# The first batch of an FFT mixing kernel: all filter pieces on one DMA queue in order of use, own tiles for split evacuations, fill work on TensorE

## The chip, the cores and the metric

The kernel runs on one core of one Trainium2 chip. The metric is the device time of one launch in microseconds (us); lower is better.

The engines go by short names. In this kernel TensorE (PE in the profiles) does the matmuls, ACT and DVE (ScalarE and VectorE) do element-wise work, GpSimd (POOL) does side work, and SP only issues transfers (DMA). The matmuls write their results to tiles in PSUM, a memory whose parts are called banks; an **evacuation** is the copy of such a tile out of PSUM by ACT or DVE. The **granted clock** (PEclk) is the share of its full clock that TensorE was given.

## The reference

```python
# x: 8 x 3008 x 256; 24064 tokens in all
X = np.fft.rfft(x, axis=1)
Y = X * (filt_r + 1j * filt_i)[None, :, :]
y = np.fft.irfft(Y, n=3008, axis=1)
# feed-forward over all tokens, d_ff = 2048
h = y.reshape(24064, 256) @ w_in
g = h * (1.0 / (1.0 + np.exp(-beta * h)))
out = g @ w_out
```

## The kernel before

The kernel does the FFT as matmuls over 3008 = 47 x 64. A batch goes through stage 1 (`s1`), a turn by transposes (`a0_turn`), stage 2 (`s2`), the product with the filters, stage 3 (`s3`), a second turn (`z_turn`) and stage 4 (`s4`; in pieces of four columns `f_0`). Batches 1 to 7 go through in small pieces while TensorE works on the feed-forward matmuls of the batch before. Batch 0 has nothing to hide behind. Its stages, and the tables that they need, make up the **opening**, which ends when the first feed-forward matmul, `hps`, starts. The change touches only the opening.

In the opening, six units of eight frequency rows by 128 channels pass through these functions. Most of these are a group of matmuls on TensorE and an evacuation of the PSUM tile by ACT or DVE (in `s2_0` the products on DVE take the evacuation's place). In the traces (Code shortened, cuts marked with dots.)

```python
spsum = pool("spsum", bufs=3, PSUM)     # tiles of two banks
tpsum = pool("tpsum", bufs=2, PSUM)     # tiles of one bank
def bank2(shape, dt=F32): return spsum.tile(shape, dt, ...)
def turn8(): return tpsum.tile([P, KH, P], BF16, ...)

def evac(dst, src, on_act, scale=None):   # ACT if on_act, else DVE
    ...

def z_turn(e, hh, on_act):                # a0_turn is built alike
    tp = turn8()
    for i in range(KH):
        nc.tensor.transpose(tp[:, i, :], zT[e][:, j0 : j0 + P], ident[:])
    evac(zz0[:, hh * KH : (hh + 1) * KH, e * P : (e + 1) * P], tp[:KP], on_act)

def s2_0(n):                              # ... 8 matmuls into ps = bank2(...)
    for c, filt in enumerate((fr_sb, fi_sb)):
        nc.vector.tensor_tensor(r_t[:], ps[:], filt[:, ks, ds], ALU.mult)
        pq[n, c] = r_t                    # the "filter products"

def s3_0(n, split=False):
    ps = bank2([P, KH, P])
    ...                                   # 8 matmuls with t3, 8 with t3s
    if split:
        for h in range(2):                # two engines, ONE tile
            evac(dst[:, js], src[:, js], h == 1)
    else:
        evac(dst, src, True)

def f_0(e, u, on_act):                    # 4 matmuls into a tpsum tile, then evac to y
    ...
def spread(n):                            # GpSimd copies a filter piece to the other half
    nc.gpsimd.tensor_copy(fr_sb[M:, ks, ds], fr_sb[:M, ks, ds])
    nc.gpsimd.tensor_copy(fi_sb[:M, ks, ds], fi_sb[M:, ks, ds])
```

The end of the opening, in program order:

```python
s2_0(4)
a0_turn(2, 1, True)
z_turn(0, 0, True); z_turn(0, 1, True)
s3_0(3); s2_0(5)
f_0(0, 0, True); f_0(0, 1, True)
z_turn(0, 2, True); z_turn(0, 3, True)
f_0(0, 2, True); f_0(0, 3, True)
s3_0(4)
f_0(0, 4, True); f_0(0, 5, True)
s3_0(5, True)                              # split
f_0(0, 6, False); f_0(0, 7, True)
z_turn(1, 0, False); z_turn(1, 1, True)
z_pair(1, 2, (False, True))
s4_0(1, 0, False); s4_0(1, 1, True); s4_0(1, 2, False); s4_0(1, 3, True)
# then the steady state: hps, gT, acc, and the plan of the later batches, e.g.
for g in range(4):
    at(o + 14 + 3 * g, load_x, 2, g)       # x of batch 2, by steps of hps
```

## Time and profile before

| | |
|---|---|
| median of 3 runs | 788.2 us (787.86 to 788.35) |
| span of the profiled run | 786.9 us |
| first filter product starts | 18.75 us |
| last filter product ends | 35.32 us |
| first `hps` starts (end of the opening) | 44.52 us |
| last group on TensorE starts | 780.99 us |

The page of the kernel before: the span, the busy time of each engine, and the chain of work that ended last by engine.

```profile
span 786.9 us, 15233 instructions
...
PE 771.1 (98%) x6063; PEld 547.6 (70%) x6063; DVE 438.1 (56%) x686; ACT 562.3 (71%) x827; POOL 155.6 (20%) x162
...
PE 95%; ACT 2%; DVE 1%; DMA 1%; issue 0%; ACTq 0%
```

TensorE (PE) is the limit over the span, and between 100 and 700 us it is busy for 599.8 of 600 us. A change of the opening therefore pays only by an earlier first `hps`, and it pays in full as long as nothing later waits.

The windows of the kernel before, three stretches of the opening. After the stretch come its length, the busy time of each engine with its instructions, the mean granted TensorE clock (PEclk, 1.00 is full), the share of DMA and the rate.

```profile
core 0: us, PE busy (x) PEld busy (x) DVE busy (x) ACT busy (x) POOL busy (x), PEclk, DMA share, GB/s
17.00:19.00 2.00, 1.85 (x19) 1.69 (x18) 2.00 (x3) 1.72 (x3) 1.94 (x3) 0.50 1.26 255
34.00:36.00 2.00, 1.91 (x20) 1.91 (x20) 1.33 (x2) 0.90 (x3) 1.94 (x4) 0.50 1.10 223
36.00:38.00 2.00, 2.00 (x29) 2.00 (x27) 0.00 (x0) 1.69 (x3) 2.00 (x2) 0.66 1.02 205
```

In all three TensorE looks busy, but at half clock or, in the third, two thirds.

The timeline of the kernel before. The columns are start and busy time in us, engine, line, operation, output and inputs, and how many instructions; in brackets the idle time just before and what ended it.

```profile
start us, us, engine line op out<-in xcount [idle before <-releaser]
...
16.53 2.29 DVE L292 TENSOR_SCALAR t3s<-t,rot 128x512 bf16<-128x512 bf16 x2
18.75 1.21 DVE L434 TENSOR_TENSOR pq_t<-sps,fr_sb 128x1024 bf16<-128x1024 f32 x1
...
28.19 1.93 ACT L113 ACTIVATE zz<-tps 96x1024 bf16<-96x1024 bf16 x2
28.36 0.61 PE L397 MATMUL tps<-ident,zT 128*128 128x128 bf16 x8 [0.29 <-ACT a L113]
...
34.11 1.21 DVE L434 TENSOR_TENSOR pq_t<-sps,fi_sb 128x1024 bf16<-128x1024 f32 x1
34.36 1.06 PE L443 MATMUL sps<-t,pq_t 128*128 128x128 bf16 x8
...
37.47 0.61 PE L443 MATMUL sps<-t3s,pq_t 128*128 128x128 bf16 x8
38.12 0.69 DVE L115 CAST zT<-sps 128x512 bf16<-128x512 f32 x1 [2.79 <-PE sps L443]
38.84 0.60 ACT L113 ACTIVATE zT<-sps 128x512 bf16<-128x512 f32 x1 [0.76 <-DVE zT L115]
...
44.52 0.59 PE L732 MATMUL hps<-y,win_sb 128*128 128x512 bf16 x2 [0.70 <-DVE y L117]
...
65.65 0.38 PE L594 MATMUL ps<-a,t 128*128 128x256 bf16 x2 [1.22 <-DMA a<-d]
```

DVE spends 2.29 us on two table rotations just before the first product. The group of eight matmuls at 34.36 us takes 1.06 us at a granted clock of 0.50; the one at 37.47 us, where the clock is back (1.00 from 37.5 us on), takes 0.61. The two halves of the last split evacuation run one after the other although they are on two engines: ACT waits 0.76 us for DVE. The last group of stage 3 (37.47 us, inputs `t3s,pq_t`) starts 2.15 us after the last product has ended, and from there it takes 7.05 us to `hps`. And in the steady state there is a wait of 1.22 us for a load.

The chain of work that ended last, three of its pieces, from the kernel before (start and length in us, what):

```profile
26.37 1.03 ACT zT L113
...
27.45 0.64 PE tps L397 x8
...
28.19 1.93 ACT zz L113 x2
```

From 17.53 to 44.52 us this chain passes through ACT's evacuations and the TensorE groups between them, and near the end through evacuations on DVE.

### The profile page before, as it was taken

How to read it: one execution, taken by the hardware profiler on the slowest of the kernel's cores; microseconds unless marked ns; L12 is line 12 of the kernel's file. 1: busy time of each engine (PE TensorE's matmuls, PEld its weight loads, DVE VectorE, ACT ScalarE, POOL GpSimd, SP SyncE). 2: the span in 40 equal slices, each digit the busy share in tenths (PEclk: the TensorE clock that was granted, in tenths of full speed). 3: DMA queues.
4: the chain of work that ended last, by engine and by line, in shares of the span. 5: the costliest groups of instructions: out<-in, count | busy, mean ns of one | idle time of the engine just before them, and what ended most of it. 6: DMA issues, size and time to landing. Idle time of an engine off the chain costs nothing.

```text
span 786.9 us, 15233 instructions
## 1 busy us (share of the span) xinstructions
PE 771.1 (98%) x6063; PEld 547.6 (70%) x6063; DVE 438.1 (56%) x686; ACT 562.3 (71%) x827; POOL 155.6 (20%) x162
## 2 busy tenths in 40 slices
PE   7799999999999999999999999999999999999997
PEld 5766767766677666876678666786667766776665
DVE  8746844776556665566655676466655566320101
ACT  6887867667666766767667776677766777777776
POOL 7823400232002220121201222012200222000000
PEclk9899999999999999999999999999999999999999
DMA  9959286233931348223480326713164211500101
GB/s 187 226 152 206 69 234 154 76 95 79 243 109 48 87 128 224 77 70 105 111 253 28 99 84 143 211 41 101 49 187 108 75 47 48 155 28 27 55 27 54
DMA packets 87066, 88.50 MB, mean 112 GB/s; under 512 B 5628, under 2 KB 77820, under 8 KB 86996
## 3 DMA queue, kind: packets, MB, share of 16 engines
q1 hardware_dynamic: 82420, 72.37, 31.1%
q0 software_dynamic: 4576, 15.17, 11.2%
q8 instruction: 47, 0.77, 0.4%
q14 instruction: 23, 0.19, 0.1%
HBM read 54.47 MB, written 46.66 MB: 129 GB/s over the span
## 4 chain that ended last, share of the span: by engine, by line
PE 95%; ACT 2%; DVE 1%; DMA 1%; issue 0%; ACTq 0%
PE acc L752 42%; PE hps L732 41%; PE ps L578 3%; PE ps L645 2%; PE ps L594 2%; PE ps L623 2%; DMA a<-d 1%; PE tps L268 1%; PE sps L443 1%; ACT zT L113 0%; ACT zz L113 0%; DVE aT L115 0%; PE tps L397 0%; DVE y L117 0%; PE tps L274 0%
## 5 line engine op out<-in xcount | busy, mean ns | idle before, releaser
L741 ACT ACTIVATE gT<-hps,beta_sb 128x512 bf16<-128x512 f32 x752 | 517.0, 687 | 208.7 <-PE hps L732 206.1
L752 PE MATMUL acc<-wout_sb,gT 128*128 128x256 bf16 x3008 | 453.4, 272 | 0.0
L732 PE MATMUL hps<-y,win_sb 128*128 128x512 bf16 (+7 forms) x1728 | 448.0, 351 | 0.9 <-DVE y L117 0.7
L752 PEld LDWEIGHTS <-gT 128*128 128x128 bf16 x3008 | 287.6, 98 | 126.1 <-issue 1.2
L613 POOL TENSOR_TENSOR yh<-a_t,b_t 128x512 bf16<-128x512 f32 x84 | 106.4, 1266 | 421.9 <-DVE b_t L612 421.0
L732 PEld LDWEIGHTS <-win_sb 128*128 128x128 bf16 x1728 | 164.9, 98 | 25.0 <-issue 1.0
L115 DVE COPY ost<-acc 128x512 f32<-128x512 f32 x93 | 59.9, 685 | 146.9 <-PE acc L752 146.9
L115 DVE CAST a<-ps 96x512 bf16<-96x512 f32 x104 | 70.8, 685 | 51.9 <-PE ps L578 47.9
L608 DVE TENSOR_TENSOR a_t<-ps,fr_sb 128x512 f32<-128x512 f32 x84 | 58.1, 692 | 72.4 <-PE ps L594 71.4
L117 DVE TENSOR_SCALAR y<-ps 128x376 bf16<-128x376 f32 x104 | 56.0, 548 | 59.3 <-PE ps L645 59.1
L609 DVE SCALAR_TENSOR_TENSOR b_t<-ps,fi_sb 64x512 f32<-64x512 f32 x84 | 58.2, 692 | 1.1
L612 DVE TENSOR_TENSOR b_t<-ps,fi_sb 64x512 f32<-64x512 f32 x84 | 57.4, 683 | 1.1
L115 DVE CAST z<-ps 128x512 bf16<-128x512 f32 x72 | 49.3, 684 | 1.7 <-PE ps L623 0.8
L645 PEld LDWEIGHTS <-zz 96*128 96x128 bf16 x448 | 29.8, 98 | 22.9
L578 PE MATMUL ps<-xg,t 94*96 94x512 bf16 x112 | 41.5, 381 | 0.0
L645 PE MATMUL ps<-t,zz 96*128 96x94 bf16 x448 | 34.7, 205 | 0.0
L594 PE MATMUL ps<-a,t 128*128 128x256 bf16 x168 | 32.1, 273 | 1.2 <-DMA a<-d 1.2
L623 PE MATMUL ps<-yh,t 128*128 128x256 bf16 x168 | 32.1, 273 | 0.0
L623 PEld LDWEIGHTS <-t 128*128 128x128 bf16 x168 | 16.3, 98 | 17.7
L594 PEld LDWEIGHTS <-t 128*128 128x128 bf16 x168 | 16.1, 98 | 16.6 <-issue 1.5
L173 POOL DMA_DIRECT2D xg<-in_x_dram x24 | 12.4, 519 | 56.5 <-PE ps L578 56.5
L578 PEld LDWEIGHTS <-t 94*96 94x96 bf16 x112 | 13.8, 123 | 10.5
(104 smaller groups left out, 194.8 us busy)
## 6 DMA issues: line engine op xcount, KB each, us to landing
out_dram<-ost SPq DMA_DIRECT2D x46, 512.0 KB, 3.0
d<-a SPq DMA_DIRECT2D x28, 384.0 KB, 4.5
a<-d SPq DMA_DIRECT2D x28, 384.0 KB, 5.5
d<-z SPq DMA_DIRECT2D x28, 384.0 KB, 3.7
zz<-d SPq DMA_DIRECT2D x28, 384.0 KB, 6.5
xg<-in_x_dram POOLq DMA_DIRECT2D x24, 384.0 KB, 6.6
ws<-in_moe_w_out_dram SPq DMA_DIRECT2D x4, 512.0 KB, 11.4
xg<-in_x_dram POOLq DMA_DIRECT2D x4, 320.0 KB, 6.2
```

Of the source, the lines that this page charges most:

```text
L115: nc.vector.tensor_copy(dst, src)
L578: nc.tensor.matmul(ps[:KP], lhsT=t1[:], rhs=xg[b, g][:NP, jj : jj + 2, :], start=True, stop=True)
L594: nc.tensor.matmul(ps[:, e, :], lhsT=t2[:, k0 + e, :], rhs=st["a2", b, g][:, kk + e, :], start=True, stop=True,)
L608: nc.vector.tensor_tensor(a_t[:], ps[:], fr_sb[:, ks, :], ALU.mult)
L609: nc.vector.scalar_tensor_tensor(b_t[:M], ps[M:], -1.0, fi_sb[M:, ks, :], ALU.mult, ALU.mult)
L612: nc.vector.tensor_tensor(b_t[M:], ps[:M], fi_sb[M:, ks, :], ALU.mult)
L613: nc.gpsimd.tensor_tensor(yh[:], a_t[:], b_t[:], ALU.add)
L623: nc.tensor.matmul(ps[:, e, :], lhsT=t3[:, 2 * i + e, :], rhs=yh[:, e, :], start=True, stop=True)
L645: nc.tensor.matmul(ps[:, e, :NP], lhsT=zz[:, j0 % JG + e, dc * P : (dc + 1) * P], rhs=t4[:], start=True, stop=True,)
L732: nc.tensor.matmul(hps[:, pos - t0 : pos - t0 + ln], lhsT=win_sb[:, dc, fb * P : (fb + 1) * P], rhs=ys[b][:, dc, n0 : n0 + ln], start=(dc ...
L741: nc.scalar.activation(gT[:], hps[:], ACT.Silu, scale=beta_sb[:, fb : fb + 1])
L752: nc.tensor.matmul(acc[tb // 2][:, tb % 2, :], lhsT=gT[:, tb * P : (tb + 1) * P], rhs=wout_sb[:, fb, :], start=(fb == 0 and tb % 2 == 0), ...
```

## The change

The intent: bring the filters in the order in which the units need them, take small work off DVE ahead of the first product, let the two halves of a split evacuation run at the same time, and keep the TensorE clock up with useless matmuls (`spin`) in the gaps. Cut to its core:

```diff
-    def load_filters(eng, k0, k1, d0, d1):        # low half on SP, high half on GpSimd
+    def load_filters(k0, k1, d0, d1):             # all 24 pieces on SP
...
-    for part in parts[:3]:
-        load_filters(nc.gpsimd, *part)
...
+    seen = sp.tile([1, 2], BF16, name="seen", tag="seen")
+    nc.sync.dma_start(seen[:], t2[:1, 1, M - 2 : M])     # an earlier gate
+    for part in parts:                                   # six parts, in order of use
+        load_filters(*part)
+    gp = nc.gpsimd
+    # rot, sgn, tiny, beta_sb, c10: from DVE to GpSimd; reciprocal: later on DVE
...
     def s1_0(g, engines):        # the same in s3_0, there by halves of k
-        ps = bank2([P, NDC, 512])
+        tiles = [bank2([P, NDC, 512])]
+        tiles.append(tiles[0] if one else bank2([P, NDC, 512]))
...
-    spin(17) ... spin(4)
+    spin(15) ... spin(5) ... spin(5) ... spin(2) ... spin(2)
...
-    a0_turn(0, 0, False); a0_turn(1, 0, True)
+    a0_turn(0, 0, False, True); a0_turn(1, 0, True, True)    # on a bank2 tile
-    t3_rotate(KH, 2 * KH, False)
+    t3_rotate(KH, 2 * KH, True)                              # DVE to ACT
...
-    a0_turn(1, 1, True)
+    a0_turn(1, 1, False)                                     # ACT to DVE
-    a0_turn(2, 1, True)
+    a0_turn(2, 1, False)                                     # ACT to DVE
...
+    s3_0(4)
     f_0(0, 2, True)
     f_0(0, 3, True)
-    s3_0(4)
-    f_0(0, 4, True)
+    f_0(0, 4, False)
+    s3_0(5, (False, True))
     f_0(0, 5, True)
-    s3_0(5, True)
     f_0(0, 6, False)
     f_0(0, 7, True)
     z_turn(1, 0, False)
     z_turn(1, 1, True)
-    z_pair(1, 2, (False, True))
+    z_turn(1, 2, False, True)
+    z_turn(1, 3, True, True)
```

## The prediction

> **What bounds the kernel now.** Over the span it is TensorE: the page gives PE 771.1 us busy of 786.9 (98%), the chain of waits is 95% PE, and the windows show PE busy for 599.8 us between 100 and 700. Nothing there changes. The change touches the first batch: the timeline starts the first feed-forward matmul (hps) at 44.52 us. All that can be won lies in those 44.5 us.
>
> **What bounds the opening.** The chain of waits passes from DVE (8.1 to 15.2 us: aT evacuations, table shifts, small operations) to a late a0 evacuation and a transpose group behind it at half clock (granted clock 0.50 in 17 to 19 us), then ACT evacuations of 1.02 us (19.7 to 34), slow TensorE again (clock 0.50 and 0.66 in 34 to 38), then a serial tail. DVE's floor is the 12 filter products, 1.21 us each, 1.13 us apart: they run from 18.75 to 35.3 us, 16.6 us for about 13.7, with waits of 0.68 and 0.29 us on GpSimd copies, themselves late by 1.36 us for a filter DMA, and 1.64 us for TensorE.
>
> **What is removed or moved.**
> 1. Small DVE operations between aT evacuations (11.66 to 13.07 us) leave DVE: 1.4 us, on the chain. Two t3s rotations (2.29 us for the pair, just ahead of the first product) go to ACT, 1.32 us for such a pair. First product at about 16.2 instead of 18.75 us.
> 2. Filters: ten issues of about 0.6 us leave GpSimd; all 24 go on SP, 0.45 us apart, from about 9.2 us (now 11.16), in order of use. [...] DMA is at its full share from 3 to 37 us, 200 to 240 GB/s, so one queue should lose no bandwidth. Estimate: 3.08 MB at 235 GB/s behind x0 (done near 12.7 us): first piece near 15, last near 26 us, now 29.2.
> 3. Two a0 evacuations go from ACT to DVE (0.69 instead of 1.02 us), into the product chain: 13.7 becomes about 15.3 us. ACT holds about 17 us of work between 16 and 33 us: slack is thin.
> 4. Own tiles for split evacuations: the last zT halves ran one after the other (38.12 to 39.44 us); in parallel this saves 0.6 us. The last aT group: about 0.5 us.
> 5. Fill matmuls (0.21 us each) keep the clock up before 15 us; they don't reach 34 to 38 us, which should shrink as waits shorten.
>
> **Sum.** Products end at about 32 instead of 35.3 us; the tail after them (9.2 us) falls to about 8. That is 4.5 us; I take off 0.6 us for new waits (GpSimd waits for t4 before spread 4; ACT and DVE both full). hps starts near 40.6 us. Gain about 3.9 us, all on the critical path since TensorE is full afterwards, unless the wait for a2 (1.2 us at 65.6) grows or xg and win_sb come late.
>
> Predicted 784.3 us, range 782.2 to 787.2. Faster by over 2%: 0.01; within 2%: 0.98; slower by over 2%: 0.01.
>
> **What would show it.** First product near 16 us, last ending near 32; GpSimd copies waiting little for filter DMA after the first; zT halves overlapping; first hps at 39.5 to 42; steady state unchanged, 0.43 us for an hps pair.
>
> **What would make it wrong.** One queue too slow for 512-byte pieces; ACT becoming the longer chain; win_sb or the first xg landing after the opening ends; the half clock returning in the tail.

## The result, and the profile after

The kernel after takes 786.28 us (785.77 to 787.35, 4 runs), the kernel before in the same rounds 788.03 us (787.23 to 788.35, 4 runs). The ratio is 0.9981 with a 95% interval of 0.9964 to 0.9998. Ratios here and below are the mean time of one kernel's fast runs over the mean of the other's fast runs of the same rounds, so not quite the ratio of the medians that are quoted. The time lies inside the forecast range; the gain is 1.75 us where 3.9 us were forecast. All outputs are right.

The page of the kernel after:

```profile
span 785.6 us, 15256 instructions
...
PE 768.7 (98%) x6071; PEld 544.7 (69%) x6071; DVE 437.1 (56%) x679; ACT 560.8 (71%) x826; POOL 151.9 (19%) x160
...
PE 94%; ACT 3%; DMA 1%; DVE 1%; issue 0%; POOL 0%; POOLq 0%; DVEq 0%; ACTq 0%
```

The share of ACT in the chain that ended last has gone from 2% to 3% of the span, and PE's from 95% to 94%. The shares are rounded, so this is a hint only; but the chain itself passes from 16.84 us to `hps` through ACT and TensorE alone.

The windows of the kernel after, the same stretches and columns as before:

```profile
17.00:19.00 2.00, 1.39 (x25) 1.20 (x23) 2.00 (x3) 2.00 (x4) 1.82 (x2) 1.00 1.22 211
34.00:36.00 2.00, 1.04 (x20) 0.93 (x20) 0.44 (x1) 1.52 (x3) 1.66 (x1) 1.00 1.06 215
36.00:38.00 2.00, 1.28 (x27) 1.17 (x25) 1.26 (x3) 1.13 (x3) 0.00 (x0) 1.00 1.06 213
```

The clock is full in all three. TensorE now idles for 0.96 us between 34 and 36 us, where before it worked slowly.

The timeline of the kernel after, columns as before:

```profile
13.96 1.15 DVE L293 TENSOR_SCALAR t3s<-t,rot 128x448 bf16<-128x448 bf16 x2
...
16.45 1.23 DVE L433 TENSOR_TENSOR pq_t<-sps,fr_sb 128x1024 bf16<-128x1024 f32 x1 [0.75 <-PE sps L428]
...
27.21 1.02 ACT L111 ACTIVATE zz<-tps 96x1024 bf16<-96x1024 bf16 x1 [0.71 <-PE tps L396]
28.28 0.61 PE L396 MATMUL tps<-ident,zT 128*128 128x128 bf16 x8 [1.11 <-ACT zz L111]
28.93 1.02 ACT L111 ACTIVATE zz<-tps 96x1024 bf16<-96x1024 bf16 x1 [0.69 <-PE tps L396]
...
31.46 1.22 DVE L433 TENSOR_TENSOR pq_t<-sps,fi_sb 128x1024 bf16<-128x1024 f32 x1
...
35.19 0.33 PE L474 MATMUL tps<-t,zz 96*128 96x94 bf16 x4 [0.96 <-ACT y L111]
35.80 0.61 PE L444 MATMUL sps<-t3s,pq_t 128*128 128x128 bf16 x8
36.23 0.69 DVE L113 CAST zT<-sps 128x512 bf16<-128x512 f32 x1
36.45 0.60 ACT L111 ACTIVATE zT<-sps 128x512 bf16<-128x512 f32 x1 [0.94 <-PE sps L444]
37.47 0.33 PE L474 MATMUL tps<-t,zz 96*128 96x94 bf16 x4 [0.72 <-ACT y L111]
37.64 1.34 PE L396 MATMUL tps<-ident,zT 128*128 128x128 bf16 x16
...
42.71 0.59 PE L726 MATMUL hps<-y,win_sb 128*128 128x512 bf16 x2 [0.89 <-ACT y L111]
...
63.79 0.38 PE L588 MATMUL ps<-a,t 128*128 128x256 bf16 x2 [1.18 <-DMA a<-d]
```

| | before | forecast | after |
|---|---|---|---|
| first product starts | 18.75 | 16.2 | 16.45 |
| last product ends | 35.32 | 32 | 32.68 |
| from there to the last stage 3 group (`t3s,pq_t`) | 2.15 | – | 3.12 |
| from there to the first `hps` | 7.05 | – | 6.91 |
| both together, the tail | 9.2 | 8 | 10.03 |
| first `hps` starts | 44.52 | 40.6 | 42.71 |
| last group on TensorE starts | 780.99 | – | 779.13 |

The first half of the forecast came true: the first product is 2.30 us earlier and the products end 2.64 us earlier. Then the tail grew by 0.83 us where it was to shrink by 1.2. The table shows where: the halves of `zT` now overlap as intended (36.23 and 36.45 us), but from the last stage 3 group on the way takes about 7 us, as before. The products are done at 32.68 us and TensorE takes them up only at 35.80. At 28.28 us TensorE waits 1.11 us for an ACT evacuation that was no obstacle in the kernel before; at 35.19 and 37.47 us it waits for ACT again. The 1.81 us at `hps` arrive at the end (1.86 us at the last group).

**The measure of the experiments.** The start of the first product differs by up to a microsecond between runs (16.2 to 17.5 us over the kernels that share its code). The two small table rotations ahead of it on DVE (128x448) start at 13.96 to 14.55 us, with the end of stage 1, and took between 0.59 us (e5, where the first GpSimd copy starts 0.06 us before they end) and 2.02 us (e4). So I compare the **stretch** from the start of the first product to the start of the first `hps`: 25.77 us before and 26.26 after. In two profiled runs of the kernel after it was 26.26 both times, in two of the kernel "e4" below 24.56 both times, in two of the kernel before 25.77 and 25.91. The forecast had it at 24.4 us (40.6 - 16.2). So the first product was off by 0.25 us and the stretch by 1.86: the stretch is where the gain was lost.

### The profile page after: what moved, and what is told of

Same layout as the page of the kernel before. It is cut to its first block, busy times and chain, and to the rows that moved or that the text cites. A ratio compares the mean times of both kernels' runs of the same rounds, so it can differ in the third digit from the quotient of the medians.

```text
span 785.6 us, 15256 instructions
## 1 busy us (share of the span) xinstructions
PE 768.7 (98%) x6071; PEld 544.7 (69%) x6071; DVE 437.1 (56%) x679; ACT 560.8 (71%) x826; POOL 151.9 (19%) x160
## 4 chain that ended last, share of the span: by engine, by line
PE 94%; ACT 3%; DMA 1%; DVE 1%; issue 0%; POOL 0%; POOLq 0%; DVEq 0%; ACTq 0%
PE acc L746 42%; PE hps L726 41%; PE ps L572 3%; PE ps L639 2%; PE ps L588 2%; PE ps L617 2%; DMA a<-d 1%; ACT zz L111 1%; ACT zT L111 1%; ACT y L111 0%; ACT aT L111 0%; PE tps L396 0%; ACT t3s L291 0%; PE sps L444 0%; ACT a L111 0%
## 5 line engine op out<-in xcount | busy, mean ns | idle before, releaser
L617 PEld LDWEIGHTS <-t 128*128 128x128 bf16 x168 | 16.2, 98 | 17.7
```

The costliest lines, as they stand in the source:

```text
L617: nc.tensor.matmul(ps[:, e, :], lhsT=t3[:, 2 * i + e, :], rhs=yh[:, e, :], start=True, stop=True)
```

## The experiments

The theories:

- **A.** The end of the opening hangs on the evacuations in ACT's queue and on the groups that stand behind them in TensorE's order. The products, the subject of the prediction, have slack.
- **B.** The products, that is DVE, still set the end.
- **C.** The order of the last groups on TensorE alone sets it.
- **D** (formed after e9). A PSUM buffer that one engine frees late sets part of it.

The kernel after and all 18 runs that gave a result:

| run | first product | last product ends | first `hps` | stretch | median us (before on that chip) | ratio to before, 95% |
|---|---|---|---|---|---|---|
| after | 16.45 | 32.68 | 42.71 | 26.26 | 786.28 (788.03) | 0.9981, 0.9964 to 0.9998 |
| e1_dve_more | 16.57 | 33.92 | 42.83 | 26.26 | 787.30 (788.04) | 1.0001, 0.9981 to 1.0021 |
| e2_act_more | 16.87 | 33.09 | 45.17 | 28.30 | 789.84 (788.04) | 1.0026, 1.0001 to 1.0050 |
| e3_s3_first | 16.82 | 33.03 | 45.90 | 29.08 | 789.63 (788.04) | 1.0024, 1.0006 to 1.0042 |
| e4_tail | 17.49 | 33.70 | 42.05 | 24.56 | 785.59 (788.04) | 0.9970, 0.9953 to 0.9987 |
| e5_two_queues | 16.21 | 32.86 | 42.72 | 26.51 | 786.14 (787.90) | 0.9990, 0.9966 to 1.0013 |
| e6_no_fill | 16.85 | 33.08 | 42.92 | 26.07 | 787.63 (787.90) | 1.0004, 0.9982 to 1.0026 |
| e7_shared | 16.39 | 32.61 | 42.73 | 26.34 | 787.06 (787.90) | 0.9997, 0.9976 to 1.0019 |
| e8_small_dve | 17.23 | 33.49 | 43.34 | 26.11 | 787.66 (787.90) | 1.0003, 0.9980 to 1.0025 |
| e9_a0_act | 16.33 | 31.73 | 41.88 | 25.55 | 786.58 (787.90) | 0.9981, 0.9969 to 0.9994 |
| e10_tail2 | 16.21 | 32.44 | 40.09 | 23.88 | 783.80 (787.90) | 0.9954, 0.9941 to 0.9966 |
| after_again | 16.38 | 32.61 | 42.64 | 26.26 | 786.17 (787.90) | 0.9982, 0.9970 to 0.9994 |
| e4_again | 16.84 | 33.06 | 41.40 | 24.56 | 784.83 (787.90) | 0.9963, 0.9950 to 0.9975 |
| e11b_alternate | 17.28 | 33.00 | 42.86 | 25.58 | 786.03 (787.51) | 0.9987, 0.9971 to 1.0003 |
| e12b_one_tile | 17.14 | 33.36 | 43.40 | 26.26 | 787.62 (787.51) | 1.0001, 0.9985 to 1.0017 |
| e13b_tail2_alt | 16.39 | 32.11 | 39.59 | 23.20 | 784.25 (787.51) | 0.9959, 0.9942 to 0.9976 |
| e14b_tail2_a0 | 17.01 | 32.42 | 40.18 | 23.17 | 784.03 (787.51) | 0.9961, 0.9945 to 0.9976 |
| before_again | 18.44 | 35.05 | 44.35 | 25.91 | 788.91 (787.26) | 1.0021, 1.0003 to 1.0038 |
| e15_later_x | 16.83 | 32.56 | 40.03 | 23.20 | 783.10 (787.26) | 0.9950, 0.9936 to 0.9963 |

### The noise first: the kernel before against itself, and the kernel after again

No edit in either.

> The kernel before, profiled a second time, to see how far one trace of it can be trusted. Expected: first product 18.5 to 19.3 us, hps 25.5 to 26.1 us after it (25.77 in the first trace), granted clock again near 0.5 in parts of 17 to 20 and 34 to 38 us; the wait for a2 of 1.2 us may be there or not.

> The changed kernel once more, on the chip of e9 and e10, as the base for both: 0.2% below the kernel before. One trace each has a jitter: the first product came at 16.45 to 17.49 us in five kernels whose code is the same up to there. Expected here: first product 16.4 to 17.5, hps 26.0 to 26.5 us after it, 10 us after the products' end.

The kernel before, run against itself, came out at 1.0021 (1.0003 to 1.0038). So a single ratio 0.2% from 1 is at the edge of what the timing can tell, and the argument below rests on the stretch in the traces; the times are its check. The gain of the change was 0.9981 once and 0.9982 the second time, in other rounds; that it is real is more likely for having come twice, but it is of the size of this error. The half clock came back in the second trace of the kernel before (0.74 in 15 to 19 us, 0.75 in 32 to 36 and 0.83 in 36 to 40, the same three means as in the first trace). Its windows show one thing that varies from run to run:

```profile
44.00:47.00 3.00, 2.65 (x7) 1.14 (x7) 0.98 (x2) 1.76 (x3) 0.00 (x0) 0.54 0.00 0
```

The granted clock was 0.54 just when the feed-forward began. The wait for the load of `a2` varies too: 1.2 us in both profiled runs of the kernel before and in the first of the kernel after, none in the second.

### e1 and e2: one more operation on DVE, one more on ACT

```diff
 # e1, in s2_0, for the last unit only: one product more, into a spare tile
+        if n == 5:
+            nc.vector.tensor_tensor(spare[:], ps[:], fr_sb[:, ks, ds], ALU.mult)
 # e2, in z_turn: the evacuation of z_turn(0, 3), on ACT, done twice
-        evac(zz0[...], tp[:KP], on_act)
+        for _ in range(2 if (e, hh) == (0, 3) else 1):
+            evac(zz0[...], tp[:KP], on_act)
```

> The changed kernel with one more DVE product of 1.22 us before the last unit's two products (its result is not used). Theory A: after the change the ACT queue and the work behind it set the end of the opening, and the products have slack there (they end at 32.68 us, their consumer starts only at 35.36). Then the products end at about 33.9 us and the first hps stays at 42.7 us within 0.3. Rival B: the product chain on DVE still sets the end. Then hps moves to about 43.9 us and the time grows by 1.2 us.

> The changed kernel with the ACT evacuation of one zz group (96x1024, about 1.0 us) done twice, at about 33 us. Theory A (ACT sets the end of the opening): first hps at 43.5 to 43.8 us instead of 42.71. Rival B (DVE products set it): hps unchanged within 0.3.

With one product more the last product ended at 33.92 us, 1.24 us later than after (1.12 later counted from the first product), and the stretch stayed at 26.26 us to the hundredth. The end of the timeline of e1:

```profile
42.83 0.59 PE L729 MATMUL hps<-y,win_sb 128*128 128x512 bf16 x2 [0.88 <-ACT y L111]
```

`hps` waits for ACT as it did. Theory B falls: the products had at least a microsecond of slack. One evacuation of 1.02 us more on ACT made the stretch 2.04 us longer. TensorE's wait for it, before the second `y` group that follows, grew from 0.51 us to 1.56: that is the operation itself. The windows of e2 show where the rest may come from:

```profile
36.00:40.00 4.00, 2.90 (x32) 2.77 (x32) 1.79 (x3) 1.96 (x5) 0.00 (x0) 0.60 1.06 213
```

The granted clock fell to 0.60 (it is 1.00 here in the kernel after). About 1.0 us is the operation itself, about 1.0 us the rest; that the rest is all clock is my reading, not a separate measurement.

### e3, e4 and e12: the order of the last groups

```diff
 # e3: the last stage 3 group right behind the one before it (after's order, one call moved)
     s3_0(4)
+    s3_0(5, (False, True))
     f_0(0, 2, True); f_0(0, 3, True); f_0(0, 4, False)
-    s3_0(5, (False, True))
 # e12: as e3, but one tile and one evacuation on DVE
-    s3_0(5, (False, True))
+    s3_0(5, (False,))
 # e4: order and engines
-    z_turn(0, 3, True)
+    z_turn(0, 3, False)
     s3_0(4)
-    f_0(0, 2, True); f_0(0, 3, True); f_0(0, 4, False)
+    f_0(0, 2, False); f_0(0, 3, False)
     s3_0(5, (False, True))
-    f_0(0, 5, True); f_0(0, 6, False); f_0(0, 7, True)
-    z_turn(1, 0, False); z_turn(1, 1, True)
-    z_turn(1, 2, False, True); z_turn(1, 3, True, True)
-    s4_0(1, 0, False); s4_0(1, 1, True); s4_0(1, 2, False); s4_0(1, 3, True)
+    f_0(0, 4, True); f_0(0, 5, True)
+    z_turn(1, 0, False, True); z_turn(1, 1, True, True)
+    z_turn(1, 2, False); z_turn(1, 3, False)
+    s4_0(1, 0, True); s4_0(1, 1, True)
+    f_0(0, 6, True)
+    s4_0(1, 2, False); s4_0(1, 3, False)
+    f_0(0, 7, True)
```

> The changed kernel with the matmuls of the last unit (s3 of unit 5) moved ahead of the three small y groups in TensorE's program, nothing moved between engines. Rival C: only the place in TensorE's order holds them up; then they start near 33.2 instead of 35.36 us and hps comes 1.5 to 2 us earlier, near 41. Theory A: they start early too, but ACT has the same work to do, so hps gains at most 0.5 us.

> The changed kernel with the order of e3 in part and with evacuations of the tail shared out anew: after the last product DVE takes one zz group, two y groups, three of the four last zz groups and two of the last y groups; ACT takes the rest. Theory A: ACT's queue ends earlier, DVE's idle 2.88 us are filled, first hps at 40.3 to 41.2 us, time 1.5 to 2.4 us below the changed kernel. Rival B: no gain, as DVE would only get more to do.

> e4 once more beside the changed kernel on one chip: 1 to 2 us below it; hps 8.4 us after the products' end against 10.0.

> e3 (last unit's matmuls moved ahead of the small y groups), but into one tile that DVE evacuates whole: one PSUM buffer and not two. Theory E: e3 lost because the second own tile had been given the bank of the unit before, still being read by ACT, so TensorE stood 1.37 us and its clock fell to half. Then here no such wait, the clock stays 1.00, and hps comes at 41.3 to 42.3 us, 1 us before the changed kernel and 4 before e3. Rival: the reorder itself is bad (the y groups come too late); then hps stays at 44 or later.

In e3 the stretch became 2.82 us longer. By itself that doesn't refute C (order alone), because a second thing went wrong. Its timeline and one of its windows:

```profile
33.42 0.39 PE L444 MATMUL sps<-t,pq_t 128*128 128x128 bf16 x4
35.18 0.38 PE L444 MATMUL sps<-t,pq_t 128*128 128x128 bf16 x4 [1.37 <-ACT zT L111]
...
40.00:44.00 4.00, 4.00 (x44) 3.90 (x43) 1.84 (x3) 2.04 (x2) 0.00 (x0) 0.54 0.47 92
```

Half of the group is done, then TensorE stands for 1.37 us. The built program says why: the second of the "own" tiles got bank 0, which is the bank of the tile of `s3_0(4)` that ACT is still reading. Afterwards the clock was 0.54.

The kernel e12 has one tile and no such wait (the group runs through from 33.74 us), but it did not come to the 41.3 to 42.3 us that I had written down: the first `hps` matmul came at 43.40 us and its second only at 44.42. The timeline of e12:

```profile
34.19 0.61 PE L444 MATMUL sps<-t3s,pq_t 128*128 128x128 bf16 x8
...
43.40 0.38 PE L726 MATMUL hps<-y,win_sb 128*128 128x512 bf16 x1
```

TensorE reached the last product 0.83 us after its end, and then needed 9.21 us to `hps`, against 6.91 after. It waited 0.74, 0.57 and 0.47 us around its small `y` groups, for ACT twice and for DVE once, and the next transposes started 20.97 us after the first product, against 21.19 in the kernel after. Up to there nothing points to a slower clock (1.00 from 32 to 36 us, and the eight `y` matmuls at 37.15 us took 0.49 us, as the eight at 34.64 took 0.50), so of the 2.30 us by which the group had come forward the order alone kept 0.22. That refutes C. Then it fell: from 36 to 40 us the mean was 0.75, and the sixteen transposes at 38.11 us took 1.86 us, those at 31.96 us 1.05. So the wait for the bank was one cause of e3's loss, the waits behind the new order another, and the half clock a third; e3's loss isn't divided between them.

In e4, where the shares of ACT and DVE were changed together with the order, the stretch became 1.70 us shorter, in two runs alike, and the times followed (ratios 0.9970 and 0.9963). `hps` came at 42.05 and 41.40 us, later than the 40.3 to 41.2 that I had expected. This fits A; new shares in the old order were not tried alone.

### e9 and e11: what moving two evacuations to DVE cost

```diff
 # e9: the two a0 evacuations back on ACT
-    a0_turn(1, 1, False)
+    a0_turn(1, 1, True)
-    a0_turn(2, 1, False)
+    a0_turn(2, 1, True)
 # e11: evacuations as in the kernel after, but the two one-bank buffers in strict turn
-    tpsum = pool("tpsum", bufs=2, PSUM)
+    tpsums = [pool(f"tpsum{i}", bufs=1, PSUM) for i in range(2)]
+    def tps_tile(shape, dt):        # used by turn8, spin and f_0
+        i = turns[0] % 2
+        turns[0] += 1
+        return tpsums[i].tile(shape, dt, ...)
```

> The changed kernel with the two a0 evacuations (a0_turn 1,1 and 2,1) back on ACT, as before. Rival B (DVE's products set the end of the opening): products end 1.4 us earlier and hps too, the time falls. Theory A (ACT sets it): products end up to 1.4 us earlier, but ACT has 2.0 us more to do against 1.85 us of idle time near 25 us: hps 0.3 to 1.5 us later.

> The changed kernel with the two small PSUM buffers of the transposes in two pools of one, taken strictly in turn. In the changed kernel the pool gave both first zz groups (z_turn 0,0 and 0,1) the same bank, 7, because the a0 group before them had gone to DVE; TensorE idled 1.11 us there for the ACT evacuation and ACT 0.69 us for TensorE. Theory D (this shared bank is what the move of a0 to DVE cost): the second zz group starts at once, near 27.4, ACT does the two back to back, hps at 41.7 to 42.1 us for a first product at 16.4 (25.3 to 25.6 us after it, against 26.26), as in e9, though the a0 evacuations stay on DVE. Rival (e9 gained because DVE had less to do): hps stays 26.1 to 26.4 us after the first product.

e9 gives ACT two more evacuations of 1.02 us, just what A says must cost. The stretch became 0.71 us *shorter* (25.55). A is not the whole truth. The timeline of e9 where it differs:

```profile
27.18 1.93 ACT L111 ACTIVATE zz<-tps 96x1024 bf16<-96x1024 bf16 x2
...
41.88 0.59 PE L726 MATMUL hps<-y,win_sb 128*128 128x512 bf16 x2 [0.89 <-ACT y L111]
```

The two `zz` evacuations run without a pause, as in the kernel before (28.19 us there). In the kernel after there are 0.69 us of idle time of ACT between them, because TensorE waits until ACT has read the first (the 1.11 us at 28.28). The built programs tell the banks that the pool gave out:

```
             z_turn(0,0)  z_turn(0,1)
before       bank 7       bank 6
after        bank 7       bank 7
e9           bank 7       bank 6
e11          bank 6       bank 7
```

In the kernel after, two tiles in direct succession share a bank, although the pool has two buffers. The pool doesn't turn strictly here; that it goes by its own guess of which is free first is how I read it, and no run shows that. e11 tests the consequence (theory D): it leaves the evacuations on DVE and only makes the buffers alternate. The timeline of e11:

```profile
28.04 2.06 ACT L111 ACTIVATE zz<-tps 96x1024 bf16<-96x1024 bf16 x2 [0.71 <-PE tps L404]
...
42.86 0.59 PE L734 MATMUL hps<-y,win_sb 128*128 128x512 bf16 x2 [0.88 <-ACT y L111]
```

The pause is gone and the stretch is 25.58 us, as in e9 (25.55). The second `zz` group starts 11.15 us after the first product instead of 11.83, and from it to `hps` it is 14.43 us in both kernels: the whole 0.68 us is won at this one wait. So the shared bank was the price of that move, and of the load of DVE or ACT nothing shows. In the times this doesn't show: e9 took 786.58 us and the kernel after 786.17 on the same chip, within the noise.

### e5, e6, e7 and e8: single parts of the change undone

```diff
 # e5: filters on two queues again (low half SP, high half GpSimd), at before's places
-    nc.sync.dma_start(dst[q0 : q0 + H, k0:k1, d0:d1], src)
+    eng.dma_start(dst[q0 : q0 + H, k0:k1, d0:d1], src)
 # e6: before's fill work
-    spin(15) ... spin(5) ... spin(5) ... spin(2) ... spin(2)
+    spin(17) ... spin(4)
 # e7: split evacuations share one tile
-    tiles = [bank2([P, KH, P])]
-    tiles.append(tiles[0] if one else bank2([P, KH, P]))
+    tiles = [bank2([P, KH, P])] * 2          # the same in s1_0
 # e8: small operations back on DVE, behind s1_0(3)
-    gp = nc.gpsimd
+    gp = nc.vector
```

> The changed kernel with the filters on two queues again (the low half of each piece on SP, the high half on GpSimd, where the kernel before had them; six pieces as in the change). The step of the prediction: one queue costs no bandwidth, and freeing GpSimd of issues brings the first product forward. Then here the first copy on GpSimd comes near 16.5 us instead of 13.7, the first product near 17.6 instead of 16.5, and the products end about 1 us later. Theory A (ACT sets the tail, products have 2.7 us of slack there): hps moves by 0 to 0.6 us. Rival: the queue change is most of the gain, hps moves by 1.5 us or more.

> The changed kernel with the fill matmuls of the kernel before (17 and 4, none later). If the fill is what keeps the granted clock at 1.00 in the whole opening, the clock falls to about 0.5 somewhere between 15 and 24 us and hps comes 0.5 to 2 us later. If the shorter waits keep it up alone, nothing changes (within 0.4 us).

> The changed kernel with the split evacuations of one tile again (both places). Own tiles were predicted to save 0.6 us at the last zT and about 0.5 us at the last aT. Theory A: the zT part is lost or nearly so, hps 0.5 to 1.2 us later. Rival: own tiles are worth nothing, as a later wait takes it back; hps within 0.3 us.

> The changed kernel with the small operations (rot, sgn, c10, tiny, reciprocal) back on DVE between the aT evacuations, 1.4 us in all. The prediction had them on the critical path: first product 1 to 1.4 us later and hps later by as much. Theory A: the first product 1 to 1.4 us later, but part of it is lost in the slack of the products, hps 0.3 to 1.2 us later.

**Queues (e5).** With two queues the first `hps` came at 42.72 us, with one at 42.71. The timeline of e5 shows the first product as its only trouble at the start:

```profile
16.21 1.22 DVE L436 TENSOR_TENSOR pq_t<-sps,fr_sb 128x1024 bf16<-128x1024 f32 x1 [0.76 <-DMA fr_sb<-in_filt_r_dram]
```

It comes 0.24 us earlier than in the kernel after, not 1.1 us later as I had expected; later one product waits 1.59 us for a GpSimd copy, which in the kernel after none does. The slack of the products absorbs both, and the stretch is 0.25 us longer only because its first end came earlier. For `hps` one queue loses nothing and gains nothing. Whether it loses bandwidth is another matter: from 15 to 19 us the kernel after moved 213 GB/s and e5 236, and the other traces divide in the same way (213 to 229 in those with one queue, 247 and 254 in the two of the kernel before). The mix of transfers in these windows differs too, so this is no clean measure.

**Fill work (e6).** Without the added fills the clock was 0.59 from 12 to 15 us and 0.88 from 15 to 19, then 1.00; in the kernel after it was 1.00 in all three. The stretch was 26.07 us, not longer. Its median is 787.63 us against 786.14 for e5 on the same chip; its profiled run, at 786.25, was the fastest of four, the others lay between 787.6 and 788.6. So it may be that in most runs the fills are worth about a microsecond that this trace doesn't show. That stays open.

**Own tiles (e7).** With shared tiles the last `zT` half was done at 37.66 us instead of 37.05 (the forecast 0.6 us), but the stretch was only 0.08 us longer. The transposes that need `zT` do start 0.55 us later in e7 (counted from the first product, 21.74 us against 21.19). But in the kernel after the second half of these transposes has to wait for an ACT evacuation of `y` (37.84 to 38.32 us) all the same, so the next group starts only 0.26 us later in e7.

**Small operations (e8).** The first product came 0.78 us later and `hps` 0.63 us later, where the forecast had 1.4 us. But the timeline of e8 puts these 0.78 us elsewhere:

```profile
14.11 1.78 DVE L293 TENSOR_SCALAR t3s<-t,rot 128x448 bf16<-128x448 bf16 x2
```

DVE reaches the two small rotations 0.15 us later than in the kernel after (13.96), and no later than other runs that have the small operations on GpSimd (14.12 to 14.14 in e2, e3, e4 and e7). Then the rotations take 1.78 us instead of 1.15, beside GpSimd's copies (13.57 to 14.60 and 14.70 to 15.74 us). That is the varying start of the first product again. So no cost of the small operations is shown at the place where e8 puts them: they fill time in which DVE of the kernel after is idle, 0.87 us before 12.62 us, waiting for TensorE.

### e10, e13 and e14: a version that wins what was forecast

```diff
 # e10: as e4, but the last stage 3 group in one tile right behind the one before,
 # and the work shared out anew
     s3_0(4)
-    f_0(0, 2, False); f_0(0, 3, False)
-    s3_0(5, (False, True))
-    f_0(0, 4, True); f_0(0, 5, True)
+    s3_0(5, (False,))
+    f_0(0, 2, True); f_0(0, 3, True); f_0(0, 4, True); f_0(0, 5, False)
     # the z_turns and s4_0(1, 0), s4_0(1, 1) as in e4, then:
-    f_0(0, 6, True); s4_0(1, 2, False); s4_0(1, 3, False); f_0(0, 7, True)
+    f_0(0, 6, False); s4_0(1, 2, False); s4_0(1, 3, True); f_0(0, 7, False)
 # e13 = e10 + e11 (strict turn);  e14 = e10 + e9 (a0 evacuations on ACT)
```

> As e4, but the last unit's matmuls go into one tile that DVE evacuates whole, right behind unit 4's, so that they need one PSUM buffer and not two (in e3 and e4 the second half waited 1.37 and 0.46 us for an ACT evacuation), and the last evacuations are shared a little otherwise. Theory A: s3 of unit 5 follows that of unit 4 with no wait, and hps comes 8.35 us after the end of the products in e4, here 7.3 to 8.0; time 0.3 to 1 us below e4, some 2.5 us below the changed kernel. If the buffer was not the cause of that wait, it stays and nothing is won over e4.

> e10 with the transposes' two PSUM buffers strictly in turn (as e11). If the gains of e10 and e11 add: hps 23.0 to 23.4 us after the first product (e10: 23.88), near 39.4; time 0.3 to 0.8 us below e10, about 4.2 below the kernel before.

> e10 with the two a0 evacuations on ACT (as e9). If the shared bank is the only cost of the move to DVE, this equals e13 within 0.3 us in the trace; if DVE's load matters too it is better, if ACT's does it is worse.

The timeline of e10:

```profile
33.27 0.61 PE L444 MATMUL sps<-t3s,pq_t 128*128 128x128 bf16 x8
33.91 1.22 DVE L113 CAST zT<-sps 128x1024 bf16<-128x1024 f32 x1 [0.89 <-PE sps L444]
...
40.09 0.59 PE L726 MATMUL hps<-y,win_sb 128*128 128x512 bf16 x2 [1.05 <-DVE y L115]
```

The last stage 3 group now starts 0.83 us after the last product (32.44 us), not 3.12, and from there it is 6.82 us to `hps`, against 6.91 after and 7.05 before. So the tail of 8 us that the prediction asked for was there to be had (7.65 us), and not by splitting the last evacuation, which here is whole again. Reaching the last product early is not enough for it: e12 reached it as early (0.83 us) and won nothing. In e10 the work behind it is shared out anew as well, and the clock stayed at 1.00 to the end of the opening. The time is 783.8 us, ratio 0.9954.

The strict turn and the a0 evacuations on ACT each shorten the stretch by 0.7 us again (23.20 and 23.17), as they did in the kernel after. Yet their times are those of e10: ratios 0.9959 and 0.9961. In the waits of e13 stands, with what waited, for what, the total, how often and the longest:

```profile
PE ps L596 <- DMA a<-d: 1.7, 1, 1.7
```

This is the load of `a2` from the table before (1.22 us there). In e13 `hps` came 0.50 us sooner than in e10, the wait for the load was 0.5 us longer, and the last group on TensorE started at the same time (776.55 and 776.58 us): the gain was given back there. In e14 the first product came late (17.01 us), so that `hps` was no sooner than in e10 (40.18 against 40.09).

### e15: the load out of the way

```diff
 # e15: e13, with the x loads of batch 2 twelve steps later
-    at(o + 14 + 3 * g, load_x, 2, g)
+    at(o + 26 + 3 * g, load_x, 2, g)
```

> e13 with the loads of x for the batch after next issued 12 steps later (step 26 on, not 14), so that the first two don't run beside the a2 loads. In e13 and e10 TensorE waited 1.7 and 1.2 us for a2 near 60 us, and e10, e13 and e14 are equally fast though hps comes at 40.09, 39.59 and 40.18 us; e4 (41.40, no wait) starts its last group of matmuls at the same 776.5 us. If that wait takes back what a still earlier hps gains, and the x loads cause it: wait below 0.6 us, last group near 775.2 to 775.8, time 0.7 to 1.4 us below e13. If the x loads are not its cause: wait and time as in e13.

The stretch is again 23.20 us, no wait for `a2` is left in the trace, and the last group on TensorE starts at 775.11 us instead of 776.55. The time is 783.1 us against 787.26 for the kernel before in the same rounds, ratio 0.9950 (0.9936 to 0.9963). This is the best version found, 4.2 us below the kernel before and clear of the noise. That it beats e13 is seen in one trace of each; their ratios overlap, and the wait was also absent in some traces of kernels that had not moved these loads (e4, twice).

## Why the prediction was right and wrong

- **What bounds the kernel: right.** The steady state didn't change, and 1.81 us at `hps` came out as 1.86 us at the last TensorE group. "All on the critical path" held, with the reserve that the prediction named: the wait for `a2` was 1.2 us in both first traces, and it took back the gain of the better versions (e13).
- **Step 1, first product near 16.2 us: right in sum** (16.45), not shown in its parts, and so perhaps by luck. DVE reaches the small rotations 1.16 us earlier than before (13.96 against 15.12), and the two large ones, 2.29 us, are gone from it. That moving the small operations brought the 1.4 us set down for it is not shown: with them back on DVE it gets there at 14.11 (e8).
- **Step 2, one queue loses no bandwidth: right for `hps`, not shown for the bandwidth.** The prediction concluded it from the share of DMA from 3 to 37 us (1.06 to 1.18 in the windows of the kernel before, 203 to 242 GB/s from 5 us on); that was my estimate. For `hps` the runs agree: 42.71 us with one queue, 42.72 with two (e5). The rate from 15 to 19 us was lower with one queue (213 against 236 GB/s), with another mix of transfers. By the same estimate one queue would gain nothing either; the prediction should have gone that step on.
- **Step 3, a0 evacuations on DVE: counted on the wrong resource.** The prediction sized them as DVE time in the product chain. The products had slack for that (e1). The cost was a PSUM bank: 0.68 us of the stretch (e11 and e9 alike).
- **Step 4, own tiles: wrong.** They removed the forecast 0.6 us from the `zT` halves, and 0.08 us from the stretch (e7). Of the 0.5 us at the last `aT` group nothing is seen: DVE reaches the next rotations at 13.96 us and with shared tiles at 14.12, where stage 1 also ended 0.16 us later.
- **Step 5, the clock: right in direction, more than forecast, the reason open.** The half clock of 34 to 38 us was to shrink "as waits shorten" and is gone (0.50 and 0.66 to 1.00), though TensorE idles more there than before (0.96 us against 0.09 between 34 and 36 us). The fills end by 15 us and are not its cause by themselves: without them it was gone too (e6: 1.00 from 32 to 40 us). How much time the full clock brought was not measured alone.
- **The sum: here the prediction failed.** The step is "the tail after them (9.2 us) falls to about 8". It measured 10.03 us. It took for granted that the tail starts when the last product ends. The runs show that it starts when TensorE gets to the last stage 3 group: 2.15 us after the last product before, 3.12 after, 0.83 in e10. From there it is 7.05, 6.91 and 6.82 us (but 9.21 in e12, so the second part isn't fixed either). TensorE gets there late because it takes groups in order and the `y` groups ahead wait for ACT (0.51 and 0.96 us in the kernel after, at 33.91 and 35.19 us); one ACT operation more at that place costs its full time and more (e2: 1.02 us more on ACT, a stretch 2.04 us longer), one DVE operation more costs nothing (e1: 26.26 us with and without). So what was won at the last product (2.64 us) was in part lost again as idle time between it and the stage 3 group, 0.97 us longer than before. The prediction had read the chain rightly up to 34 us ("ACT evacuations of 1.02 us (19.7 to 34)"), had seen "slack is thin" on ACT, and had named ACT as a risk; but its sum runs over the products, which were not on that chain, and has no term for ACT.

In numbers: of the 1.86 us by which the stretch missed its forecast, 0.68 is the shared bank, and about 0.5 is own tiles that were to save 0.6 and saved 0.08. The bank acts mostly before the last product ends: with it mended the tail is still 9.86 us (e11). The rest, about 0.7 us by subtraction, is assigned by no run; order and shares together are worth more than that (2.38 us in e10). The parts were measured one at a time and need not add up exactly.

## What to carry to other kernels

When an operation on one engine ends earlier, look for the group that consumes it in the *order* of the next engine, and ask what that engine waits for before it gets there; the gain can stop at such a wait (here 2.64 us at the last product were 1.81 at `hps`). Moving the group forward is not enough if the groups behind it then wait for the same engine (e12: 9.21 us from there to `hps` instead of 6.91). After moving an evacuation to another engine, look at which buffers the pool hands out afterwards, because two successive tiles in one bank can undo the pipelining of a pool of two (TensorE stood 1.11 us for it in the kernel after). And when a stage ends sooner, look whether the wait for the next load has grown, before concluding that the gain was not real.

## What the traces show of the clock, the banks and the work beside GpSimd

- The clock. In the kernel before, groups of eight follow each other at 0.44 us with a granted clock of 1.00 (28.36 to 29.70 us) and at 0.85 with 0.50 (34.36 to 36.06), and that half clock stood from 34 us into the half microsecond after 37 (0.96 in 33.5 to 34 us, 0.50 up to 37, 0.62 in 37 to 37.5, then 1.00). The longest gap on TensorE doesn't tell the cases with a fall from the one without: in the kernel before it fell at 34 us when no gap in the six microseconds ahead was over 0.82 us, in e3 between 36 and 40 us (0.61) after a longest gap of 1.37, and in the kernel after it stayed at 1.00 behind a gap of 1.11 us (28.28 us). The busy time of TensorE in the windows of four microseconds that were asked for doesn't either: it was 2.02 us in 30 to 34 us, ahead of the fall, in the kernel before; in 32 to 36 us it was 2.14 in e2, 2.63 in e3 and 3.26 in e12, with 0.60, 0.61 and 0.75 in the next four microseconds, and 2.53 in the kernel after, with 1.00. So no rule follows from these few cases.
- The banks. A pool of two buffers handed out the same bank twice in succession; that cost 1.11 us of TensorE time and 0.68 us of the stretch (after against e11). In e3 a pool of three gave a tile the bank that ACT was still reading, which cost 1.37 us of TensorE time.
- DVE beside GpSimd. In the kernel after, the first of the two 128x448 rotations took 0.90 us and ended 0.15 us after the copy that ran beside it, the second took 0.33. The pair took 0.59 us in the kernel before, with no GpSimd copy beside it, 1.15 us in the kernel after and 1.78 us in e8, beside GpSimd copies; in e7 it took 0.60, though a copy ran beside its first 0.21 us. ACT did the larger 128x512 pair in 1.33 us (kernel after), where DVE needed 2.29 in the kernel before, beside two such copies. Why the rotations take longer there isn't shown.
